# Tiny reads of x, w_mod and wqkv issued before the first real loads of a transformer block

## The chip, the cores and the metric

The kernel runs on one core of a Trainium2 chip. The metric is the device time of one execution in microseconds (us). The profile covers a slightly shorter span than the timed execution: 241.8 us of span belong to 243.6 us of time.

Names: PE is TensorE, DVE is VectorE, ACT is ScalarE, POOL is GpSimd, SP is SyncE; a "q" behind a name is that engine's instruction sequencer, which issues the DMAs. "Queue" means the list of DMAs that one engine issues.

## The reference, cut to what matters

```python
mod = (silu(c) @ w_mod).reshape(B, 6, 1, D)            # B=2, N=256, D=1152
shift_a, scale_a, gate_a, shift_m, scale_m, gate_m = ...
h = layernorm(x) * (1 + scale_a) + shift_a
q, k, v = split(h @ wqkv)                              # two heads
x = x + gate_a * (softmax(q k^T) v @ wo)
h2 = layernorm(x) * (1 + scale_m) + shift_m
out = x + gate_m * (gelu(h2 @ w_fc1) @ w_fc2)
```

Before the first large matmul can start, the core needs layernorm statistics of x (four tiles of 128 rows, tiles 0 and 1 from batch 0, tiles 2 and 3 from batch 1) and `scale_a`, which is a product of silu(c) with a part of w_mod.

## The kernel before

The loads, in the order of issue (cuts are marked):

```python
nc.scalar.dma_start(c_sb[:], c_v)                       # 4.5 KB, ACT's queue
for t in (0, 1, 3, 2):                                  # 288 KB each, SP's queue
    nc.sync.dma_start(x_sb[:, t, :], x_v[:, t // TPB, t % TPB, :])
...
nc.gpsimd.memset(sT[:], 0.0)
...
for k0, k1 in SGROUPS:                                  # then weights, SP's queue
    nc.sync.dma_start(w_scale_a[:, :, k0*P:k1*P], wmod_v[...])
    ...  # w_k pieces
```

The head of the compute. PE ran its matmuls in the order of the program:

```python
warm(2, pwarm)                                          # fp32 matmuls on zeros
nc.tensor.transpose(pc[:], c_sb[:], ident[...])         # waits for c
nc.scalar.activation(sig[:], pc[:], ACT.Exp, scale=-1.0)
...  # three small DVE operations: sT = silu(c)
warm(7, pwarm)
act_stats(0)                                            # ACT: two passes over tile 0
for j in range(NPD): stats_piece(1, j)                  # DVE: statistics of tile 1
...
act_stats(2)                                            # ACT: two passes over tile 2
...
pt_a = transpose_x([0, 1], BT[0])                       # PE: batch 0 (tiles 0, 1)
...
pm0, pm1 = [scale_group(k, k + 1, acc_tile) for k in range(2)]  # PE: needs w_scale_a
...  # first k matmuls, batch 0
transpose_x([0, 1], [2], pt_c, 0)                       # PE: tile 2
```

## Time and profile before

| | before |
|---|---|
| time, median of 3 | 243.78 us (243.64 to 244.18) |
| PE busy | 235.4 us, 97% of the span |
| c landed | 2.86 us |
| x tiles 0, 1, 3, 2 landed | 3.63, 4.74, 6.12, 7.19 us |
| first w_scale_a piece landed | 9.17 us |
| PE's transpose of tile 2 starts | 11.41 us |

A DMA has "landed" when the last of its DMA engines has counted up its semaphore; these times come from the semaphore records of the trace.

The page of the kernel before, the busy times and the chain that ended last:

```profile
PE 235.4 (97%) x1688; PEld 144.4 (60%) x1698; DVE 91.5 (38%) x193; ACT 59.9 (25%) x121; POOL 28.3 (12%) x47
PE 94%; issue 2%; ACT 2%; POOL 1%; DVE 0%; POOLq 0%; DVEq 0%; ACTq 0%
```

PE is the bound. After the head it has hardly a gap, so anything that starts PE's first useful work later goes straight into the time.

The timeline of the kernel before, first 12 us (start in us, duration in us, engine, line, operation, tiles; in brackets the idle time before it and what ended it):

```profile
0.73 0.62 ACTq L84 DMA_DIRECT2D c_sb<-in_c_dram  x1
...
3.18 0.19 PE L176 MATMUL pc<-ident,c_sb 18*128 18x18 bf16 x1
...
3.30 4.29 PE L173 MATMUL pwarm<-zeros 128*128 128x256 f32 x14
...
3.66 1.25 ACT L206 ACTIVATE sink<-x_sb 128x1152 f32<-128x1152 bf16 x1
...
4.76 1.48 DVE L193 BATCH_NORM_STATS2 stats<-x_sb 128x6 f32<-128x384 bf16 x3 [0.31 <-DMA x_sb<-in_x_dram]
...
8.82 0.40 PE L264 MATMUL pt<-ident,xn 128*128 128x128 bf16 x4 [1.23 <-DVE xn L233]
...
9.26 0.60 PE L247 MATMUL pm<-sT,w_scale_a 128*128 128x2 bf16 x18
...
11.41 0.28 PE L264 MATMUL pt<-ident,xn 128*128 128x128 bf16 x2 [0.29 <-DVE xn L233]
```

PE takes c at 3.18. And `pm`, the product with w_scale_a, starts at 9.26, 0.09 us after its weights have landed.

### The profile page before, as it was taken

Reading aid. Unit: us, or ns where it says so; the run is one execution under the profiler, and the core shown is the slowest. Engines: PE = TensorE matmul, PEld = TensorE weight load, DVE = VectorE, ACT = ScalarE, POOL = GpSimd, SP = SyncE. Lnnn points to the kernel's source line nnn. Section 1 sums busy time; section 2 is a strip of 40 time slices with the busy share of each in tenths; the row PEclk is TensorE's granted clock in tenths of the full one; section 3 lists DMA queues with packets and bytes.
Section 4 is the critical chain, followed back from the end, with each engine's and each line's share of the span. In section 5 each row is a group of like instructions: output and inputs, shape, how many; then the busy total and the mean of one; then the engine's idle time right before and its main releaser. Section 6 shows DMA issues by size and latency. Waiting matters only on the chain.

```text
span 241.8 us, 3979 instructions
## 1 busy us (share of the span) xinstructions
PE 235.4 (97%) x1688; PEld 144.4 (60%) x1698; DVE 91.5 (38%) x193; ACT 59.9 (25%) x121; POOL 28.3 (12%) x47
## 2 busy tenths in 40 slices
PE   8799999999999999999999999999999999999994
PEld 5585444465567566888844444444556665566674
DVE  3742442319325678830002999960010000000001
ACT  6633322307215032671422333222000000000000
POOL 2300000002300324100000000001121111111111
PEclk9999999999999999999999999999999999999999
DMA  6999999997579999239999999999200000000000
GB/s 188 327 317 310 378 366 393 389 391 247 147 263 398 387 377 159 49 59 361 391 391 391 340 327 284 274 327 284 98 16 16 20 16 16 19 18 19 27 23 16
DMA packets 48781, 53.29 MB, mean 220 GB/s; under 512 B 9587, under 2 KB 36475, under 8 KB 48763
## 3 DMA queue, kind: packets, MB, share of 16 engines
q1 hardware_dynamic: 41312, 50.14, 62.5%
q10 hardware_dynamic: 6939, 1.71, 4.7%
q0 software_dynamic: 512, 1.19, 1.5%
q8 instruction: 13, 0.21, 0.4%
q14 instruction: 5, 0.04, 0.0%
HBM read 50.14 MB, written 1.19 MB: 212 GB/s over the span
## 4 chain that ended last, share of the span: by engine, by line
PE 94%; issue 2%; ACT 2%; POOL 1%; DVE 0%; POOLq 0%; DVEq 0%; ACTq 0%
PE pacc L799 29%; PE pacc L743 29%; PE pacc L690 7%; PE pacc L599 7%; PE pq L521 7%; PE pk L280 5%; PE pk L309 2%; PE pa L639 2%; PE ps_s L556 2%; PE pn L416 2%; ACT sink L206 1%; PE pt L264 1%; PE pm L247 1%; PE pg L498 0%; ACT rstd L335 0%
## 5 line engine op out<-in xcount | busy, mean ns | idle before, releaser
L743 PE MATMUL pacc<-hT,w_f 128*128 128x256 bf16 (+1 forms) x427 | 70.3, 325 | 0.3
L799 PE MATMUL pacc<-w_f,gT 128*128 128x384 bf16 (+2 forms) x468 | 70.5, 314 | 0.0
L799 PEld LDWEIGHTS <-gT 128*128 128x128 bf16 x468 | 44.4, 98 | 26.2
L743 PEld LDWEIGHTS <-w_f 128*128 128x128 bf16 x432 | 42.2, 98 | 27.6
L805 DVE TENSOR_TENSOR tmp<-pacc,gate 128x384 f32<-128x384 f32 (+2 forms) x13 | 6.9, 527 | 65.6 <-PE pacc L799 57.2
L775 ACT ACTIVATE gT<-pacc 128x512 bf16<-128x512 f32 x24 | 14.3, 597 | 32.6 <-PE pacc L743 32.6
L469 DVE SCALAR_TENSOR_TENSOR part<-w_gate_m,s,part 128x1152 f32<-128x1152 bf16 x16 | 21.4, 1414 | 0.0
L807 POOL TENSOR_TENSOR o_sb<-tmp,x 128x384 bf16<-128x384 f32 (+1 forms) x12 | 11.7, 973 | 54.0 <-DVE tmp L805 54.0
L690 PE MATMUL pacc<-w_o,big 128*128 128x384 bf16 x108 | 17.9, 326 | 0.0
L521 PE MATMUL pq<-hT,w_q 128*128 128x512 bf16 x79 | 17.7, 379 | 0.1
L599 PE MATMUL pacc<-w_v,hT 128*128 128x384 bf16 x108 | 17.7, 326 | 0.0
L599 PEld LDWEIGHTS <-hT 128*128 128x128 bf16 x108 | 10.5, 98 | 7.1 <-issue 0.3
L690 PEld LDWEIGHTS <-big 128*128 128x128 bf16 x108 | 10.4, 98 | 7.2 <-issue 0.4
L521 PEld LDWEIGHTS <-w_q 128*128 128x128 bf16 x81 | 7.9, 98 | 9.4
L280 PE MATMUL pk<-big,w_k 128*128 128x256 bf16 (+1 forms) x70 | 13.1, 324 | 0.1
L696 POOL TENSOR_TENSOR x<-tmp,x_sb 128x384 f32<-128x384 f32 x8 | 7.3, 914 | 27.4 <-DVE tmp L695 27.4
L467 DVE TENSOR_SCALAR part<-w_gate_m,s 128x1152 f32<-128x1152 bf16 x2 | 1.6, 818 | 22.3 <-DMA w_gate_m<-in_w_mod_dram 22.3
L491 POOL DMA_DIRECT2D gates_dram<-nat_v x2 | 1.1, 536 | 67.7 <-DVE nat_v L489 67.7
L280 PEld LDWEIGHTS <-w_k 128*128 128x128 bf16 x72 | 6.7, 97 | 3.7 <-issue 0.3
L764 ACT ACTIVATE gT<-pacc 128x512 bf16<-128x512 f32 x12 | 6.5, 598 | 8.9 <-PE pacc L743 8.9
L512 POOL DMA_DIRECT2D gates_dram<-nat x4 | 2.3, 584 | 49.3 <-DVE nat L509 48.7
L695 DVE TENSOR_TENSOR tmp<-pacc,gate 128x384 f32<-128x384 f32 x12 | 6.6, 549 | 3.1 <-PE pacc L690 3.1
(102 smaller groups left out, 164.2 us busy)
## 6 DMA issues: line engine op xcount, KB each, us to landing
w_f<-in_w_fc_dram SPq DMA_DIRECT2D x12, 864.0 KB, 14.9
w_f<-in_w_fc_dram SPq DMA_DIRECT2D x3, 1728.0 KB, 7.9
w_f<-in_w_fc_dram SPq DMA_DIRECT2D x2, 2592.0 KB, 17.2
w_gate_a<-in_w_mod_dram SPq DMA_DIRECT2D x3, 864.0 KB, 11.9
w_v<-in_wqkv_dram SPq DMA_DIRECT2D x3, 864.0 KB, 13.8
w_o<-in_wo_dram SPq DMA_DIRECT2D x3, 864.0 KB, 14.0
w_shift_m<-in_w_mod_dram SPq DMA_DIRECT2D x3, 864.0 KB, 6.6
w_scale_m<-in_w_mod_dram SPq DMA_DIRECT2D x3, 864.0 KB, 12.1
```

The lines of the kernel that those rows point to most:

```text
L280: nc.tensor.matmul(pk[m][:, c0:c1], w_k[:, k, m * P:(m + 1) * P], hT0[:, k, c0:c1], start=(k == 0 and c0 == 0), stop=(k == KD - 1), skip_g ...
L469: nc.vector.scalar_tensor_tensor(part[:, b, :], wg[:, k, :], s32[:, k, b:b + 1], part[:, b, :], op0=ALU.mult, op1=ALU.add,)
L521: nc.tensor.matmul(pq[m][:], w_q[:, k, m * P:(m + 1) * P], hT[:, k, :], start=(k == 0), stop=(k == KD - 1), skip_group_check=True,)
L599: nc.tensor.matmul(pacc[:], hT[:, k, t * P:(t + 1) * P], w_v[:, k, pnl * PW:(pnl + 1) * PW], start=(k == 0), stop=(k == KD - 1),)
L690: nc.tensor.matmul(pacc[:], aT[:, k, t * P:(t + 1) * P], w_o[:, k, c0:c1], start=(k == 0), stop=(k == KD - 1),)
L695: nc.vector.tensor_tensor(tmp[:], pacc[:], gate_a[:, b, c0:c1], op=ALU.mult)
L696: (nc.gpsimd if pool_add else nc.vector).tensor_tensor(x1[:, t, c0:c1], tmp[:], x_sb[:, t, c0:c1], op=ALU.add)
L743: nc.tensor.matmul(dst, w_f1[m // KD][:, k, ml * P:(ml + 1) * P], hT[:, k, c0:c1], start=start, stop=(k == KD - 1), **kw,)
L775: nc.scalar.activation(gT[:, m, :], pacc[:], ACT.Gelu_apprx_tanh)
L799: nc.tensor.matmul(pacc[:], gT[:, kk, t * P:(t + 1) * P], w_f2[j][:, r, c0 - n * PW:c0 - n * PW + cw], start=(kk == 0), stop=(kk == KF - 1),)
L805: nc.vector.tensor_tensor(tmp[:], pacc[:], gate_m[:, b, c0:c0 + cw], op=ALU.mult)
L807: (nc.vector if last else nc.gpsimd).tensor_tensor(o_sb[:], tmp[:], x1[:, t, c0:c0 + cw], op=ALU.add)
```

## The change

The DMA records of the trace show that most 2304-byte reads of x take 93 ns, but some of them take 0.2 to 1.4 us. The intent is to take the first read of an address range out of the real loads: 16 small groups of 64-byte reads, meant to be one for each of the 16 DMA engines, go to ranges that are read in full later. One such load goes on ACT's queue ahead of c (batch 1's x), two go on POOL's queue (w_mod and wqkv).

```diff
     c_sb = act.tile([B * KD, P], BF16, name="c_sb")
+    touch_x = act.tile([16, 2, 32], BF16, name="touch_x")
+    nc.scalar.dma_start(touch_x[:], x.rearrange("b (e r) d -> e b r d", e=16)[:, 1, 0:16:15, 0:32])
     nc.scalar.dma_start(c_sb[:], c_v)
@@
     nc.gpsimd.memset(sT[:], 0.0)
+    touch_w = act.tile([16, KD + 2, 32], BF16, name="touch_w")
+    nc.gpsimd.dma_start(touch_w[:, 0:KD, :], wmod_v.rearrange("(e r) k n -> e r k n", e=16)[:, 0, :, D:D + 32])
+    nc.gpsimd.dma_start(touch_w[:, KD:KD + 2, :], wqkv_v.rearrange("(e r) k n -> e r k n", e=16)[:, 0, 0:2, D:D + 32])
```

Nothing reads the two touch tiles.

## The prediction

> **What bounds the kernel now.** The page gives PE 97% busy of a 241.8 us span at a granted clock of 0.998. From 11.41 us on the chain of waits is PE almost without a gap, so only the first 11 us can give or lose anything. The timeline there:
> - c lands at about 2.9 us (16th count of its semaphore); PE's transpose of it starts at 3.18, ACT's exponential at 3.41.
> - x tile 0 lands at 3.63, and ACT's first statistics pass starts at 3.66.
> - From there the chain is ACT: two passes of 1.25 us plus reads, POOL 0.24, ACT root and exponential, then (7.52 to 10.05) two passes over tile 2, DVE normalise at 10.94, PE transpose at 11.41. ACT is not waiting for the later x tiles: they land at 4.74, 6.12 and 7.19, and tile 2 is read at 7.52.
> - Weights: the first w_scale_a piece lands at 9.17 and is used at 9.26, the first w_k row block at 9.69 and 9.84. Hidden behind ACT.
>
> **What the change is after.** In the DMA records most 2304-byte reads of x take 93 ns, but about 34 of them take 0.2 to 1.4 us; those after 3.4 us (20, batch 1) cost about 0.5 us per engine. First reads of the weights show only some four such stalls (0.24 to 0.29 us). So the touch of x can pull tile 2's landing forward by perhaps 0.3 to 0.8 us; the touches of the weights have almost nothing to remove.
>
> **What it adds.**
> - One DMA issue on ACT's queue ahead of c: c's own issue took 0.62 us, x's 0.42 us each. I estimate c leaves 0.4 to 0.6 us later.
> - Stalls now come first. c's 256-byte reads took 15 ns each, but on three engines they finished only at 2.83, after long x reads on (apparently) the same engines: a stalled read holds up the other queue. The Trainium skill (DMA: Bandwidth & Descriptors, "Issuing engines are not separate DMA queues") says queues share the same 16 engines; this trace agrees. So the touches' stalls will delay c and x tile 0, the two that are critical, to relieve tiles 2 and 3, which are not.
> - Two issues on POOL, about 0.55 us each by the gate stores' durations. POOL is idle from 2.5 to 6.6 us: free. About 13 tiny descriptors per engine: under 0.4 us of DMA time.
> - Semaphore slots rotate by one: no effect.
>
> **Critical path.** ACT's first statistics pass starts 0.2 to 1.0 us later, and the whole chain and PE shift with it. The gain in x tiles 2 and 3 and in the weights lands in slack and is worth about 0.
>
> **Prediction.** 244.2 us (243.4 to 245.1): a small loss of about 0.4 us. Faster by over 2%: 0.01; within 2%: 0.98; slower by over 2%: 0.01.
>
> **What the profile would show.** c landing 0.3 to 1 us later; ACT's first pass starting at 3.9 to 4.6 instead of 3.66; long x reads after tile 1 fewer; tile 2 landing at or before 7.2; PE's transpose at 11.41 moved by the same amount as ACT's start; POOL's two issues done before 5 us.
>
> **What would make it wrong.** If stalls on one queue do not hold the other, x tile 0 keeps 3.63 and c's delay falls below 0.2 us: no change. If tile 0's own stalls vanish too, the kernel gains up to 0.5 us. If the touches stall much longer than the reads they replace, or POOL's issues run past 6.6 us, the loss exceeds 1 us.

## The result, and the profile after

| | before | after |
|---|---|---|
| time, median of 4 | 243.71 us (243.63 to 244.18) | 243.91 us (243.60 to 244.19) |
| ratio | | 1.0007, 95% interval 0.999 to 1.0023 |
| c landed | 2.86 us | 3.56 us |
| x tiles 0, 1, 3, 2 landed | 3.63, 4.74, 6.12, 7.19 | 3.49, 4.20, 5.96, 7.56 |
| first w_scale_a piece landed | 9.17 us | 9.61 us |
| PE's transpose of tile 2 starts | 11.41 us | 11.50 us |

A ratio is the mean time of one kernel's fast runs over that of the other's of the same rounds, so it is not quite the ratio of the medians quoted. The two kernels count as the same.

The same two lines of the page after:

```profile
PE 236.7 (98%) x1688; PEld 145.1 (60%) x1698; DVE 91.3 (38%) x193; ACT 60.1 (25%) x121; POOL 29.4 (12%) x49
PE 91%; DMA 5%; DVE 1%; SPq 1%; ACT 1%; issue 0%; DVEq 0%; ACTq 0%
```

The timeline after, the same operations and the added issues:

```profile
0.73 0.41 ACTq L85 DMA_DIRECT2D touch_x<-in_x_dram  x1
...
1.17 0.59 ACTq L86 DMA_DIRECT2D c_sb<-in_c_dram  x1
...
1.55 0.74 POOL L100 DMA_DIRECT2D touch_w<-in_w_mod_dram  x1
...
3.61 0.19 PE L181 MATMUL pc<-ident,c_sb 18*128 18x18 bf16 x1 [0.36 <-DMA c_sb<-in_c_dram]
...
3.73 5.38 PE L178 MATMUL pwarm<-zeros 128*128 128x256 f32 x14
...
3.92 1.25 ACT L211 ACTIVATE sink<-x_sb 128x1152 f32<-128x1152 bf16 x1
...
4.73 1.47 DVE L198 BATCH_NORM_STATS2 stats<-x_sb 128x6 f32<-128x384 bf16 x3
...
8.94 0.39 PE L269 MATMUL pt<-ident,xn 128*128 128x128 bf16 x4
...
9.66 0.60 PE L252 MATMUL pm<-sT,w_scale_a 128*128 128x2 bf16 x18 [0.22 <-DMA w_scale_a<-in_w_mod_dram]
...
11.50 0.28 PE L269 MATMUL pt<-ident,xn 128*128 128x128 bf16 x2
```

PE now waits for c inside its warm-up (0.36 us), the 14 warm-up matmuls take 5.38 instead of 4.29 us, and PE waits for w_scale_a. In this profile the chain that ended last goes through that load (start, us, what):

```profile
2.56 7.05 DMA w_scale_a<-in_w_mod_dram
9.61 0.05 issue
9.66 0.60 PE pm L252 x18
```

(The rest of the page's 5% for DMA is `hT<-xn` at 93.85 us, see below.) Yet this head is only 0.09 us longer at the transpose of tile 2. By the first q matmul it is 0.20 us behind (32.38 before, 32.58 after).

The two profiled spans differ by 0.6 us (241.8 and 242.4), and most of that is not in the head. It appears at the first MLP matmul. Before, then after:

```profile
96.98 0.60 DVE L662 TENSOR_SCALAR hT<-hT,scale_m,shift_m 128x256 bf16<-128x256 bf16 x2 [0.26 <-DMA hT<-xn]
...
97.62 1.58 PE L743 MATMUL pacc<-hT,w_f 128*128 128x256 bf16 x13
```

```profile
97.89 0.60 DVE L667 TENSOR_SCALAR hT<-hT,scale_m,shift_m 128x256 bf16<-128x256 bf16 x2 [0.98 <-DMA hT<-xn]
...
98.29 0.92 PE L748 MATMUL pacc<-hT,w_f 128*128 128x256 bf16 x7 [0.31 <-DVE hT L667]
```

There DVE waits for a DMA that transposes the normalised x, and PE waits for DVE. From the first wo matmul to the first MLP matmul it took 97.62 - 77.63 = 19.99 us before and 98.29 - 77.83 = 20.46 after. The experiments show that this term goes up and down by itself, between 19.98 and 20.81 us; 20.81 is from a run of the kernel before. It must be left out when two heads are compared. So the table below gives the start of the first q matmul, "q start": from there to the first wo matmul every profile of that table, whatever the kernel, took 45.24 to 45.25 us.

### The profile page after: what moved, and what is told of

Read it like the earlier page. It is cut to its first block, busy times and chain, and to the rows that moved or that the text cites. A ratio compares the mean times of both kernels' runs of the same rounds, so it can differ in the third digit from the quotient of the medians.

```text
span 242.4 us, 3983 instructions
## 1 busy us (share of the span) xinstructions
PE 236.7 (98%) x1688; PEld 145.1 (60%) x1698; DVE 91.3 (38%) x193; ACT 60.1 (25%) x121; POOL 29.4 (12%) x49
## 3 DMA queue, kind: packets, MB, share of 16 engines
q10 hardware_dynamic: 6987, 1.71, 5.2%
## 4 chain that ended last, share of the span: by engine, by line
PE 91%; DMA 5%; DVE 1%; SPq 1%; ACT 1%; issue 0%; DVEq 0%; ACTq 0%
PE pacc L804 29%; PE pacc L748 29%; PE pacc L604 7%; PE pq L526 7%; PE pk L285 5%; PE pacc L695 4%; DMA w_scale_a<-in_w_mod_dram 3%; PE pk L314 2%; PE pa L644 2%; PE ps_s L561 2%; DMA hT<-xn 2%; PE pn L421 2%; PE pm L252 1%; PE pt L269 1%; SPq L88 1%
## 5 line engine op out<-in xcount | busy, mean ns | idle before, releaser
L178 PE MATMUL pwarm<-zeros 128*128 128x256 f32 x18 | 7.5, 589 | 1.2 <-DVE eps_t L95 1.2
```

Source lines behind the costliest of these rows:

```text
L178: nc.tensor.matmul(dst[:, 0:T // 2], zeros32[:, 0:P], zeros32, start=True, stop=True)
```

## The experiments

Twelve runs were made in four jobs. The theories, as they stood at the start:

- Theory A: the touch of x makes tile 1 land earlier, the delayed c cancels that at DVE's first statistics, and the touch of the weights delays w_scale_a.
- Rival B: the touches do nothing to the other loads; landing times vary between executions.
- Later rivals: C (what delays c is the first read of batch 1's x) and D (the loss comes by way of the DMA engines or landing times, and c has slack or only goes along).

The columns of this table are read from the traces: c landed; the end of the warm-up, which is PE's transpose start or the modelled end of the last warm-up matmul; the first w_scale_a piece landed; `pm` start; q start; mean time minus the mean time of all runs of the kernel before in the same job.

| run | c | warm-up ends | w_scale_a | pm | q start | time difference |
|---|---|---|---|---|---|---|
| before (first profile) | 2.86 | 7.59 | 9.17 | 9.26 | 32.38 | |
| e5_before (same kernel) | 2.86 | 8.25 | 9.02 | 9.06 | 32.55 | +0.10 |
| e4_x_after_c | 2.89 | 8.18 | 9.28 | 9.32 | 32.22 | +0.06 |
| e11_before_c_deferred | 2.86 | 8.46 | 9.57 | 9.62 | 32.53 | +0.07 |
| e3_w_only | 2.87 | 7.84 | 9.19 | 9.24 | 32.17 | +0.57 |
| e12_w_again (same as e3) | 2.86 | 8.35 | 10.49 | 10.54 | 33.45 | +0.81 |
| after (first profile) | 3.56 | 8.94 | 9.61 | 9.66 | 32.58 | +0.09 |
| e1_after (same kernel) | 3.66 | 9.96 | 9.95 | 10.41 | 33.07 | +0.39 |
| e2_x_only | 3.71 | 9.59 | 9.59 | 10.02 | 32.66 | +0.36 |
| e6_sham | 3.72 | 9.74 | 9.54 | 10.16 | 32.82 | +0.21 |
| e10_after_c_deferred | 3.65 | 8.73 | 9.91 | 9.95 | 32.87 | +0.42 |
| e7_four | 5.49 | 11.41 | 8.41 | 11.84 | 34.49 | +2.34 |

The upper six have no DMA ahead of c, the lower six have one or more.

### e1_after: the changed kernel again

No edit.

> The changed kernel once more, with enough rounds to see how often each of two times comes up. Both kernels have shown only two times so far, near 243.6 us and near 244.2 us, three and one (before) and two and two (after). Theory A (the change moves the head by 0.1 to 0.2 us and the 0.6 us between the two times comes from a straggling DMA engine later on, in both kernels): both times appear for both kernels, and the ratio of means stays within 0.9995 to 1.002. Rival B (the change itself causes the slower time): after is near 244.2 in most runs, before near 243.6 in most, ratio 1.002.

Measured: 244.16 us median (243.96 to 244.35, six runs) against 243.79 (243.20 to 244.59, eleven runs), ratio 1.0014 (0.9999 to 1.0029). There were not two times: the runs of before fill the range evenly, and the two values seen at first were chance. The ratio sits where A put it, but A's reason does not hold, as the next runs show.

The most telling view here is the chain of waits of this run, in order of time (start, us, what):

```profile
1.18 2.48 DMA c_sb<-in_c_dram
...
3.71 0.19 PE pc L181
3.90 6.25 PE pwarm L178 x14
10.15 0.22 PE pt L269 x4
10.38 0.10 PE pm L250
10.48 0.54 PE pm L252 x18
```

The chain does not go through ACT or DVE. It goes from c's landing through PE's own warm-up matmuls. Here are the warm-up matmuls by line, before and then in this run (times in ns min/median/max):

```profile
L173 PE MATMUL pwarm<-zeros x18: 379/432/796, 1.2 to 7.2; 128*128 128x256 f32 x18
```

```profile
L178 PE MATMUL pwarm<-zeros x18: 617/634/796, 1.2 to 9.5; 128*128 128x256 f32 x18
```

The same 18 matmuls are all slow in this run, and half of them are fast before. By the start times of the records, the 14 follow each other every 427 ns in this run; before, every 427 ns until 5.2 us, and every 216 ns from 5.5 us on.

### e2_x_only: the touch of x alone

```diff
+    touch_x = ...                      # as in the change
+    nc.scalar.dma_start(touch_x[:], ...)
     nc.scalar.dma_start(c_sb[:], c_v)
                                        # no touch_w
```

> Only the touch of batch 1's x, ahead of c. Theory A (x tile 1 lands earlier because of the touch, c lands later, and the two cancel at VectorE's first statistics; the touch of the weights is what delays the first w_scale_a piece): c used by PE at 3.5 to 3.7 us, x tile 1 landed at 4.1 to 4.4, first VectorE statistics at 4.6 to 4.8, first w_scale_a piece landed by 9.2, PE's transpose of tile 2 at 11.3 to 11.5; time equal to before within 0.2 us. Rival B (landing times of x vary from execution to execution and the touch does nothing): x tile 1 lands near 4.7, first w_scale_a piece anywhere from 9.1 to 9.7.

Measured: ratio 1.0013 (0.9999 to 1.0028). c was used by PE at 3.76, tile 1 landed at 4.40, DVE's first statistics started at 4.89, w_scale_a landed at 9.59, PE's transpose of tile 2 started at 11.71. A's range for that transpose (11.3 to 11.5), for w_scale_a (by 9.2) and for DVE (4.6 to 4.8) are all missed, and the loss of 0.36 us is above its 0.2.

```profile
3.76 0.19 PE L178 MATMUL pc<-ident,c_sb 18*128 18x18 bf16 x1 [0.51 <-DMA c_sb<-in_c_dram]
...
3.88 5.87 PE L175 MATMUL pwarm<-zeros 128*128 128x256 f32 x14
...
9.59 0.39 PE L266 MATMUL pt<-ident,xn 128*128 128x128 bf16 x4
...
10.02 0.60 PE L249 MATMUL pm<-sT,w_scale_a 128*128 128x2 bf16 x18
```

PE goes from warm-up to transpose to `pm` without a wait: the warm-up decides. And the slow reads of x that the touch was meant to remove were all there: 29 records after 3.3 us that took over 180 ns, 12.2 us above 93 ns in sum, against 23 records and 8.6 us in the first profile of before. But this profile is the exception. By the same count the five others with a touch of x (after, e1, e4, e7, e10) have 2.8 to 4.8 us, and the six without one (before, e3, e5, e6, e11, e12) 4.5 to 11.5 us. So the touch of x may well have removed slow reads; single profiles do not show it, and the times show no gain from it.

### e3_w_only and e12_w_again: the touches of the weights alone

```diff
     nc.gpsimd.memset(sT[:], 0.0)
+    touch_w = ...                      # both touches of the weights, as in the change
```

> Only the touches of w_mod and wqkv on the gpsimd queue. Theory A (they stall single DMA engines by 0.5 to 1 us and give nothing back): c as before (PE at 3.2), x tile 1 at 4.7 or later, touch reads with single records of 0.4 to 1.0 us, first w_scale_a piece landed at 9.4 to 9.8 with one engine last by more than 0.4 us, PE waiting for it; PE's transpose of tile 2 at 11.4 to 11.6; time 0 to 0.3 us above before. Rival B (the w touch is harmless, the straggling engine has another cause): first w_scale_a piece by 9.2 and no difference to before.

Measured: 244.36 us median, but from 243.36 to 245.53; ratio 1.0022 (0.9996 to 1.0048). The profile fell on the fastest run and looks like before, with w_scale_a landing at 9.19 and one touch record of 0.53 us. It could not say what the slow runs do, so the same kernel was run once more.

> The touches of the weights alone, once more. The first set of its runs spread from 243.36 to 245.53 us and its profile fell on the fastest of them. Theory A (the touch of w_mod sometimes holds single engines for 0.5 to 2 us, as in both profiles of the changed kernel): at least one record of that touch over 0.5 us, first w_scale_a piece landed at 9.2 to 10.0 us, mean time 0 to 0.5 us above before. Rival B (the spread was chance): mean within 0.15 us of before, spread no wider than that of before.

Measured: 244.29 us median, 243.49 to 246.47; ratio 1.0031 (0.9997 to 1.0066). This profile (a run of 244.65 us) shows it:

```profile
8.50 1.26 ACT L209 ACTIVATE sink<-x_sb 128x1152 f32<-128x1152 bf16 x1 [1.20 <-DMA x_sb<-in_x_dram]
...
10.54 0.60 PE L250 MATMUL pm<-sT,w_scale_a 128*128 128x2 bf16 x18 [1.53 <-DMA w_scale_a<-in_w_mod_dram]
```

Three records of the touch of the weights lasted 0.79, 1.28 and 1.80 us. One DMA engine then counted up last in all that follows: tile 2 landed at 8.47, where the last but one engine was done at 7.25, and w_scale_a at 10.49 against 9.32. A tile is complete only with its slowest engine, so one engine held for a microsecond delays every load behind it. Over both sets 6 of 12 runs were above 244.5 us; of the 33 runs of before in the three jobs with rounds, and six more as e5_before, 2 of 39 were. A's account of these touches holds in this profile, and its expectation of 10.0 us for w_scale_a was even passed. The intervals of both ratios still reach 1, because the runs scatter.

### e4_x_after_c: the touch of x behind c

```diff
+    touch_x = ...
     nc.scalar.dma_start(c_sb[:], c_v)
+    nc.scalar.dma_start(touch_x[:], ...)
```

> The touch of x moved behind c on the same queue, no touch of the weights. Theory A (c's delay is what eats the gain of the touch): PE takes c at 3.2, x tile 1 landed by 4.4, first VectorE statistics at 4.3 to 4.5 instead of 4.76, PE's transpose of tile 2 at 11.0 to 11.2 unless the first w_scale_a piece, landed at about 9.1, holds PE; time 0.1 to 0.4 us under before. Rival B (touch does nothing to x): head as before, transpose of tile 2 at 11.4, time equal.

Measured: ratio 1.0001 (0.9982 to 1.002). PE took c at 3.19, DVE started at 4.42, PE's transpose of tile 2 at 11.07, all as A said, but the time was not below before. The next run tells why.

### e5_before: the kernel before against itself

No edit.

> The kernel before against itself: how far two sets of runs of one kernel differ, and how much the head varies from one profiled execution to another. If the landing times of x vary on their own (rival B), this profile shows x tile 1 anywhere from 4.3 to 4.8 us and PE's transpose of tile 2 anywhere from 11.0 to 11.8. If they are set by the order of the loads (theory A), it repeats 4.74 and 11.41 within 0.1. Ratio within 0.999 to 1.001.

Measured: ratio 1.0006 (0.9986 to 1.0026), 243.38 to 244.55 us.

```profile
3.18 0.19 PE L176 MATMUL pc<-ident,c_sb 18*128 18x18 bf16 x1
...
3.30 4.95 PE L173 MATMUL pwarm<-zeros 128*128 128x256 f32 x14
...
4.38 1.48 DVE L193 BATCH_NORM_STATS2 stats<-x_sb 128x6 f32<-128x384 bf16 x3
...
11.03 0.29 PE L264 MATMUL pt<-ident,xn 128*128 128x128 bf16 x2
```

In this execution of the unchanged kernel tile 1 landed at 4.36, and PE's transpose of tile 2 started at 11.03. So 4.74 and 11.41 in the first profile were one late engine's doing in one execution (15 engines had tile 1 by 4.38). Theory A took that for the rule and the 4.20 after for the touch's gain; it falls, and rival B is right on this point. Against 11.03 here and 11.07 in e4_x_after_c, the lower six of the table start tile 2's transpose at 11.50 to 13.53; but the other four of the upper six do so at 11.13 to 12.41, so this start alone does not separate the groups. The head of e5_before also shows a further term: its q start was 32.55 in spite of the early 11.03, because PE waited 0.37 us at 19.7 us for a later piece of w_scale_a.

### e6_sham: the same small load from somewhere else

```diff
-    nc.scalar.dma_start(touch_x[:], x.rearrange(...)[:, 1, 0:16:15, 0:32])
+    nc.scalar.dma_start(touch_x[:], wo.rearrange("(e r) n -> e r n", e=16)[:, 0:72:71, 0:32])
```

(ahead of c, no touch_w)

> The touch of x replaced by one of the same shape and queue that reads 64-byte pieces of wo, which nothing else reads for 50 us. Theory A (a DMA ahead of c costs its issue and its own wait whatever it reads, and delays c and the chain behind it): c used by PE at 3.5 to 3.8 us, as with the real touch, first VectorE statistics at 4.7 to 4.9, time 0.2 to 0.4 us above before. Rival C (what delays c is the first read of batch 1's x): c used at 3.2 to 3.4, time as before.

Measured: c landed at 3.72 and was used at 3.76, DVE's first statistics started at 4.89, exactly as with the real touch in e2_x_only; warm-up ended at 9.74; ratio 1.001 (0.9991 to 1.003), +0.21 us. C is refuted in its first part: c is delayed by a small DMA ahead of it, whatever that reads. Its time alone does not separate the two.

### e7_four: four touches ahead of c

```diff
+    touch_x = act.tile([16, 4, 2, 32], BF16, name="touch_x")
+    for i in range(4):                 # written out as four lines
+        nc.scalar.dma_start(touch_x[:, i], x.rearrange(...)[:, 1, 0:16:15, 32*i:32*i+32])
     nc.scalar.dma_start(c_sb[:], c_v)
```

> Four touches of batch 1's x (neighbouring 64-byte pieces) ahead of c instead of one. Theory A (c is on the chain that starts the statistics: c, PE transpose, ScalarE, VectorE's sT, then VectorE's first statistics): c used at 4.7 to 5.2 us, first VectorE statistics about 1.2 us after c, so 5.9 to 6.3, PE's transpose of tile 2 at 12.5 to 13.0, time 1.0 to 1.7 us above before. Rival D (c has slack, the head is set by the landing of x and of the first w_scale_a piece): time within 0.4 us of before.

Measured: 246.04 us median, ratio 1.0098 (1.008 to 1.0117), +2.34 us, the one clear difference.

```profile
5.53 0.19 PE L181 MATMUL pc<-ident,c_sb 18*128 18x18 bf16 x1 [2.28 <-DMA c_sb<-in_c_dram]
...
5.65 5.92 PE L178 MATMUL pwarm<-zeros 128*128 128x256 f32 x14
...
11.41 0.39 PE L269 MATMUL pt<-ident,xn 128*128 128x128 bf16 x4
...
11.84 0.60 PE L252 MATMUL pm<-sT,w_scale_a 128*128 128x2 bf16 x18
```

D is refuted in its plain form: with four touches ahead of it, c has no slack. A's direction is right and its size is not (c later than 5.2, time above 1.7 us). c landed 2.63 us later than before, and each of the three further touches cost about 0.6 us of that ((5.49 - 3.71) / 3). w_scale_a had landed at 8.41, so it was not the bound here: PE's warm-up was.

### e8_x_twice and e9_other_first: does a first read stall?

```diff
+    first = act.tile([P, NT, D], BF16, name="first", tag="big")
+    first_v = x_v                      # e9: the first 512 rows of w_fc2, same shape
+    for t in (0, 1, 3, 2):
+        nc.sync.dma_start(first[:, t, :], first_v[:, t // TPB, t % TPB, :])
     for t in (0, 1, 3, 2):
         nc.sync.dma_start(x_sb[:, t, :], ...)
```

> All four x tiles are first loaded into an unused tile and then loaded again, so the second reads find addresses that were read some 5 us earlier. The kernel is slower by about 4 us; only the DMA records matter. Theory A (a first read of an address range stalls an engine): in the first pass some 30 to 40 reads of 2304 bytes over 180 ns, 10 us or more of excess in all; in the second pass under 8 of them and under 2 us. Rival B (the stalls belong to the time after the start, or to other traffic): the second pass has a third or more of the first pass's excess.

> The same, but the first pass reads the first 512 rows of w_fc2, of the same shape, so x is read for the first time in the second pass. Theory A (first reads stall): stalls in both passes, the second pass with 4 us of excess or more, above all when batch 1 begins. Rival B (stalls belong to the start of the program): stalls in the first pass only, the second as quiet as in the run that reads x twice.

One profile each; these kernels are slower on purpose. Of the 2304-byte records, in order of their start, 512 to a pass:

| | over 180 ns | their sum above 93 ns |
|---|---|---|
| e8, first pass (x, first time) | 31 | 11.2 us |
| e8, second pass (x again) | 16 | 2.9 us |
| e9, first pass (w_fc2, first time) | 39 | 13.3 us |
| e9, second pass (x, first time) | 24 | 5.9 us |

Both theories are half wrong. x read for the first time costs 5.9 us when it is read in the second pass (e9) and 11.2 us in the first (e8), so about half of the excess belongs to the first 6 us of the program and not to the address. (The first pass of e9 does not tell: it too reads its addresses for the first time.) x read for the first time in the second pass costs 3.0 us more in sum than x read again, and of that 2.6 us are in its first 128 records, batch 0. Batch 1, which the change touches, costs the same read first (1.46 us) or again (1.48 us). With one profile each this is only an indication that a touch of batch 1 has little to remove, and the sums under e2_x_only point the other way. What makes reads slow in the first 6 us stays open.

### e10_after_c_deferred and e11_before_c_deferred: c's work later in the order

```diff
-    (ACT exponential of c, three DVE operations for sT, ahead of the statistics)
     act_stats(0)
+    (ACT exponential of c)
     ...
     norm1(0, 0, CUT)
+    (three DVE operations for sT)
```

> The changed kernel with the work on c moved later in program order: ScalarE's exponential of c behind its two statistics passes over tile 0, VectorE's three operations on it behind the first two normalisations. Theory A (the touch costs time only because c stands ahead of the statistics in the order of ScalarE and VectorE): c still lands at 3.5 to 3.7 us, but the first ScalarE pass starts at 3.5 to 3.7 and the first VectorE statistics at 4.2 to 4.5 (x tile 1's landing), the first q matmul starts at 32.2 to 32.5 us instead of 32.6 to 33.1, time 0.2 to 0.4 us under the changed kernel and level with before. Rival D (the loss comes through the DMA engines, c only goes along): the first q matmul stays at 32.6 or later.

> The same reordering on the kernel before, without touches: what the reordering is worth alone. Theory A: c landed at 2.9 us was ready in time, so nothing is gained; ScalarE's exponential now costs about 0.2 us on its chain; first q matmul at 32.2 to 32.6 us, time within 0.3 us of before. If it is 0.3 us or more under before, c was costing time already.

Measured: e10 ratio 1.0016 (0.9998 to 1.0034); e11 ratio 1.0002 (0.9987 to 1.0016). In e10:

```profile
3.67 1.25 ACT L203 ACTIVATE sink<-x_sb 128x1152 f32<-128x1152 bf16 x1 [0.59 <-DMA x_sb<-in_x_dram]
...
3.70 0.19 PE L181 MATMUL pc<-ident,c_sb 18*128 18x18 bf16 x1 [0.45 <-DMA c_sb<-in_c_dram]
...
4.42 1.48 DVE L190 BATCH_NORM_STATS2 stats<-x_sb 128x6 f32<-128x384 bf16 x3 [3.29 <-DMA x_sb<-in_x_dram]
...
9.95 0.60 PE L244 MATMUL pm<-sT,w_scale_a 128*128 128x2 bf16 x18 [0.73 <-DMA w_scale_a<-in_w_mod_dram]
```

ACT and DVE start as early as A asked (3.67 and 4.42), and nothing is won: q start stays at 32.87, where A asked for 32.2 to 32.5 and D for 32.6 or later. In this profile w_scale_a, landed at 9.91 with touch records of 0.59 and 0.76 us before it, holds PE, so it cannot show what ACT's and DVE's wait for c is worth alone. That PE was not held by this wait is read from the other profiles, below. e11 shows that the reordering itself costs nothing that the times show.

No version beat both kernels. e4_x_after_c, the best candidate, is level with before.

## Why the prediction was right or wrong

**The time.** Predicted 244.2 us (243.4 to 245.1), a loss of 0.4 us; measured 243.91, and 244.16 in the second set, with ratios 1.0007 and 1.0014, which at 243.8 us are 0.2 and 0.3 us. Both intervals include no change. "Within 2%" held. The mean q start of the five profiles with one small DMA ahead of c (two of them without the touch of the weights) is 32.80, that of the four with neither such a DMA nor a touch of the weights 32.42, so the head loses about 0.4 us. The forecast of the size came out, in part by luck: of its reasons, the later c is right, and the stalls and the way by ACT, below, are not. No single ratio is clear of no change; the ten runs of the changed kernel taken together, each set against the runs of before in its job, are slower by an estimated 0.29 us, with a standard error of 0.12.

**"c leaves 0.4 to 0.6 us later": right, and c lands later still.** c was issued 0.44 us later (1.17 against 0.73) and landed 0.70 to 0.86 us later in the five profiles. In the records c's first reads came at 1.71 before, and at 2.91 after, when the touch's reads (2.30 to 2.75) were through; both stand on ACT's queue. Why the touch's own reads come only at 2.1 to 3.0 where it stands ahead of c, with x or with wo as source, is open.

**"Stalls now come first ... the touches' stalls will delay c and x tile 0": this step failed for the touch of x.** Its 64-byte reads took 11 ns each in every profile, and x tile 0 landed at 3.49 in the first profile after and at 3.65 to 3.74 in the four others, against 3.63 and 3.66 in the two of before. c was late because it stood behind another DMA on its own queue, whatever that one read (e6_sham). The prediction rested here on the Trainium skill, page DMA: Bandwidth & Descriptors, section "Issuing engines are not separate DMA queues", which says that DMAs from different issuers share the same 16 engines. For the touches of the weights the trace of e12 agrees: with a record of 1.80 us on POOL's queue, one engine was late in the loads of SP's queue (8.47 against 7.25). The records do not name the engine, so that it is the same one is inferred.

**"ACT's first statistics pass starts later, and the whole chain shifts with it": this step failed.** ACT did start later, 3.92 against 3.66, but PE was not waiting for it: in the lower six profiles x of batch 0 was normalised 0.21 to 1.13 us before PE came to transpose it, and in e1, e2, e6 and e7 the transpose of tile 2 follows the start of `pm` by 1.69 to 1.70 us of PE's own work. In the table, `pm` follows the end of the warm-up by 0.42 to 0.45 us (e1, e2, e6, e7), or w_scale_a's landing by 0.04 to 0.05 us (after, e10, and four of the upper six; in the other two, the first profile and e5, by 0.09 and 0.04, with PE's transposes of x only just done), whichever is later. So two things held PE: its own warm-up, and the landing of w_scale_a.

What each is worth can be estimated from the table. Where `pm` follows w_scale_a, q start comes 22.90 to 22.93 us after `pm`; where it follows the warm-up, 22.64 to 22.66 us, since PE then waits less further on. Had the warm-up never been the later of the two, q start would be about 0.05 + 22.91 us after w_scale_a's landing, on average at 32.68 in the five profiles with one small DMA ahead of c. So of the 0.38 us between 32.80 and 32.42 about 0.12 us came by the warm-up and 0.26 us by w_scale_a, which landed at 9.72 on average against 9.26. The slow touches of the weights can account for that in after, e1 and e10; in e2 and e6, without them, 9.59 and 9.54 are hardly later than the 9.57 of e11, which has no touch at all. That the touch of x delays w_scale_a is therefore not shown. Only in e7_four is the loss the warm-up's alone.

**What the prediction overlooked: a wait inside a warm-up.** Without a DMA ahead of c, PE had some 0.13 us without work before c's transpose (the fourth warm-up matmul starts at 2.62 and takes a step of 0.43, so 3.05 to 3.18). With one, PE was without work from 3.05 to between 3.61 and 3.76, with four until 5.53. The records of the granted clock then put the change to the full clock at 5.37, 5.86, 6.54, 6.70, 6.89 and 7.12 us in the six upper rows, and at 7.47, 7.99, 9.44, 10.00 and 11.02 us in five of the lower ones. (e2_x_only has no such record; there the spacing of the matmuls changes at 9.2 us.) The two groups do not overlap. e8_x_twice and e9_other_first, also without a DMA ahead of c, have 6.71 and 4.59. Seven warm-up matmuls, issued as 14, that run at half clock for longer end later: 7.59 to 8.46 us in the upper rows, 8.73 to 11.41 in the lower.

The Trainium skill explains why a half-microsecond wait can cost more than itself. Page TensorE: Matmul & The Clock Gate, section "Part 1: The HAM clock gate", says that the clock doubles after a busy window of 3413 ns, and that the window is free-running. The trace agrees: the recorded stretches at full clock last 235.52 and 232.106 us, which is 69 and 68 times 3.4133 us; e8 has shorter stretches of 3.413 and 6.827 us, and the spacing of the matmuls changes where the records say. The change to full clock then ends a window. In after, e1, e2, e6 and e7 the window before it contains the wait for c; it did not count, and another 3.41 us had to pass. In e10 that window also contains PE's idle start, before 1.18 us, so e10 would probably have been as late without the wait. With a free-running window, where in it a program starts is chance: in the eight profiles without a DMA ahead of c the full clock came anywhere from 4.59 to 7.12 us. The nearest thing to a pair is e9 and after: the window from 1.18 to 4.59 us counted in e9, with 0.13 us without work in it, and the one from 1.16 to 4.58 us did not count in after, with 0.56 us. That the wait causes the late clock is inferred from this pair and from the split of the groups. A kernel with the touch and with c's transpose behind all the warm-up matmuls, which would test it directly, was not run.

**"The touches can pull tile 2's landing forward by perhaps 0.3 to 0.8 us": not in the changed kernel.** Tile 2 landed at 7.19 and 7.05 in the two profiles of before, and at 7.56 and 7.96 in the two of the changed kernel, where one engine was late: the last but one was done at 6.73 and 7.03, against 7.04 and 6.94. Long x reads were fewer, as the prediction said (15 and 18 over 180 ns after 3.3 us, against 23 and 24). About half of the excess of the reads that it counted as "first reads" belongs to the first 6 us (e8, e9).

**"POOL ... free", "about 13 tiny descriptors per engine: under 0.4 us of DMA time": wrong.** POOL's issues were indeed done by 2.85 us and harmless. The reads were not: single records of 1.03 us (after), 1.92 us (e1_after), 0.53 us (e3), 0.76 us (e10) and 1.80 us (e12), with one engine late behind them in the worst cases. Why the slowest runs, up to 246.47 us, came with the touches of the weights alone, and the changed kernel stayed below 244.4 in its ten runs, is open.

**Semaphore slots: "no effect".** Nothing in the traces speaks against it.

## What to carry to other kernels

When an engine runs in program order, look for waits in the places where it is only warming up: here half a microsecond of waiting went, in four of five profiles with one small DMA ahead of c, with one more clock window of 3.41 us at half clock. What that costs depends on what PE would have waited for anyway: by the estimate above only 0.12 of 0.38 us, because w_scale_a came late too. A small load is not small when it stands ahead of one that something waits for, and a load is as late as its slowest DMA engine. Before explaining half a microsecond by a change, profile the unchanged kernel twice and find the terms that move by themselves; here one of them, late in the kernel, was as large as the whole effect.

## What the Trainium skill lacked or had wrong

- TensorE: Matmul & The Clock Gate: it names idle gaps of some 3 us, and frequent short ones, as the danger, and asks for a window of sustained work. It lacks how long a single gap may be for a window still to count. Here windows with 0.13 us without work counted, and windows with 0.53 to 0.71 us in one piece did not (inferred, as said above).
- DMA: Bandwidth & Descriptors: it gives about 2 us as the fixed cost of one DMA (fitted for the gpsimd path), but no cost for the DMA behind it on the same queue. Here one small DMA made c land 0.70 to 0.86 us later, though its issue took only 0.42 us, and further ones about 0.6 us each.
- DMA: Bandwidth & Descriptors: apart from a general range for the latency of HBM, it has nothing on how long a tiny read from POOL's queue can hold up loads of other queues. Here single records of 576 bytes or less, mostly 29 ns or less, took 0.5 to 1.9 us.
- None has the slow reads at the start of a program: 31 and 39 of 512 reads took over 180 ns in the first pass, 16 and 24 in the second.
